# Strassen's seven products for the second product of eight chunks, a ring for x, and earlier scores

## The chip, the cores and the metric

One core of one Trainium2 chip. The metric is the device time of one execution in microseconds (us), as a median of several executions; lower is better. A run is called slow when it lies over 1.5% above the fastest of its kernel.

## The reference, cut to what matters

```python
# attention: q, k, v of shape (8, 8, 576, 64); heads 0-3 a window of 32 keys, heads 4-7 every 4th of 128
scores = scale * np.matmul(q, k.transpose(0, 1, 3, 2))
scores = np.where(masks[None], scores, -1000000000.0)
attn = softmax(scores)
x = (attn @ v).transpose(0, 2, 1, 3).reshape(4608, 512)
# two products with a squared relu between
h = x @ w_in            # (4608, 512) @ (512, 2048)
r = np.maximum(h, 0.0)
return (r * r) @ w_out  # (4608, 2048) @ (2048, 512)
```

## The kernel before

The 4608 tokens are nine chunks of 512. A chunk's first product is 64 matmuls of 128x512, each tile of it followed by a relu on ScalarE and a square on VectorE (into `g`, fp16); its second product is 64 matmuls again. Attention is done in eight "rows" b (one batch element each). From row 2 on, row b is interleaved with chunk b-1: the two products are a generator, and `pump(n)` issues n steps of it (two matmuls of 512 columns a step, 0.43 us) between small groups of attention work. In the traces an engine takes its instructions in the order of issue (below, a reciprocal of VectorE whose input was complete at 82.6 us starts at 85.41, behind four instructions issued ahead of it), so the place of a `pump` decides what waits behind what.

```python
def mm1_gen(c, g):
    xs = xT[:, :, c * TOKC : (c + 1) * TOKC]
    for ffc in range(NFF):                       # 16
        ph = pmool.tile([P, TOKC], FP32, ...)
        for dmk in range(NDM):                   # 4
            nc.tensor.matmul(ph, wi4[...], xs[:, dmk, :], ...)
            if dmk == 1: yield
        rt = osb.tile(...)
        nc.scalar.activation(rt, ph[:], ACTF.Relu)
        nc.vector.tensor_mul(g[:, ffc, :], rt, rt)
        yield

def mm2_gen(c, g):
    for t in range(TOKC // P):                   # 4 tiles of 128 tokens, 16 matmuls each
        po = pmool.tile([P, DM], FP32, ...)
        for ffc in range(NFF):
            mm2(c, g, po, t, ffc)
            if ffc % 2 == 1 and ffc < NFF - 1: yield
        store(c, t, po); yield
# ...
for b in range(2, B):
    pending.append(moe_gen(b - 1))
    last = b + 1 == B
    if not last:
        after_transposes(b)            # GpSimd waits until row b's transposes have landed
        ns = load_sliding_qk(b + 1)    # GpSimd's DMA queue
        if b == 2: cast_v(b)           # GpSimd
        dd = keep_dilated_qk(b + 1)
        load_v(b + 1)
        nr = by_token(b + 1, ns)       # GpSimd, the copy "nr<-ns"
        cast_v(b + 1)                  # GpSimd
    pump(24)
    attn_scores(b, 4)                  # 4 groups, 4 steps after each
    if not last:
        dp = keep_sliding_qk(b + 1, nr)    # SyncE's DMA queue, to DRAM
    attn_values(b, 2)                  # 9 groups, 2 steps after each
    if not last:
        transpose_dilated(b + 1, dd)   # SyncE's DMA queue
        transpose_sliding(b + 1, dp)
    pump(1000)
```

The chain that prepares the next row: the transposed keys of row b land, then GpSimd loads q and k of row b+1, copies them by token (`nr`), SyncE's queue writes them to DRAM (`dp`) and transposes them into `QKTp`, and only then can row b+1's scores begin. Row 2 holds GpSimd's casts of v for two rows, its own and row 3's.

The softmax here doesn't subtract the row's maximum and nothing guards it: scores larger than these inputs give would overflow.

## Time and profile before

The median is 322.25 us (322.08 to 323.05, three runs). The profiled execution has a span of 318.3 us. A "row of attention" below runs from the first matmul of one chunk's first product to that of the next. "Hole-free" is the row with attention and nothing that waits, 32.37 us in this trace.

| part of the trace before | us |
|---|---|
| before chunk 1 | 62.80 |
| rows 2, 3 | 32.72, 32.79 |
| rows 4, 5, 6 | 32.5, 32.8, 33.0 |
| row 7 (no work of GpSimd) | 32.37 |
| chunks 7 and 8 alone | 27.63, 27.79 |

Rows 2 to 6 together are 2.0 us longer than five hole-free rows. The prediction shows the windows of rows 3, 6 and 7. Row 2 looks like this (its window, like those of the prediction, is set about one matmul later than the first one, which changes no length by more than 0.02 us; stretch, its length, busy time and instruction count of PE, PEld, DVE, ACT, POOL, then granted clock, DMA share, GB/s):

```profile
62.98:95.70 32.72, 32.47 (x269) 17.18 (x268) 17.04 (x38) 18.36 (x32) 13.90 (x22) 1.00 1.09 230
```

GpSimd has the most to do of all rows (22 instructions), yet VectorE, with half of the row free, loses little, and neither does TensorE.

### The profile page before, as it was taken

Reading aid. Unit: us, or ns where it says so; the run is one execution under the profiler, and the core shown is the slowest. Engines: PE = TensorE matmul, PEld = TensorE weight load, DVE = VectorE, ACT = ScalarE, POOL = GpSimd, SP = SyncE. Lnnn points to the kernel's source line nnn. Section 1 sums busy time; section 2 is a strip of 40 time slices with the busy share of each in tenths; the row PEclk is TensorE's granted clock in tenths of the full one; section 3 lists DMA queues with packets and bytes.
Section 4 is the critical chain, followed back from the end, with each engine's and each line's share of the span. In section 5 each row is a group of like instructions: output and inputs, shape, how many; then the busy total and the mean of one; then the engine's idle time right before and its main releaser. Section 6 shows DMA issues by size and latency. Waiting matters only on the chain.

```text
span 318.3 us, 6260 instructions
## 1 busy us (share of the span) xinstructions
PE 302.9 (95%) x2484; PEld 157.8 (50%) x2484; DVE 162.2 (51%) x353; ACT 168.7 (53%) x286; POOL 79.2 (25%) x119
## 2 busy tenths in 40 slices
PE   1899989999999999999999999999999999999995
PEld 1455544454555445545555455555554555445542
DVE  5683548447543674369435952596256525203400
ACT  2726635568436834684368536762577256316611
POOL 4192018403480361137012800371000000000000
PEclk9999999999999999999999999999999999999999
DMA  7999998999999993998399839984810110010011
GB/s 126 197 155 215 207 210 144 195 257 192 211 259 224 205 270 100 217 194 184 106 205 184 191 91 216 191 172 126 173 44 1 68 68 0 27 72 36 1 66 66
DMA packets 79213, 46.67 MB, mean 147 GB/s; under 512 B 54352, under 2 KB 72784, under 8 KB 79184
## 3 DMA queue, kind: packets, MB, share of 16 engines
q1 hardware_dynamic: 64928, 31.60, 40.8%
q0 software_dynamic: 14256, 14.68, 28.1%
q8 instruction: 19, 0.31, 0.4%
q14 instruction: 10, 0.08, 0.1%
HBM read 39.85 MB, written 16.52 MB: 177 GB/s over the span
## 4 chain that ended last, share of the span: by engine, by line
PE 68%; DMA 12%; DVE 7%; SPq 5%; POOL 3%; issue 2%; ACT 2%; POOLq 0%; ACTq 0%
PE ph L259 31%; PE po L274 31%; SPq L120 4%; DMA wi<-in_moe_w_in_dram 4%; DVE AT L381 3%; DMA sd<-in_v_dram 2%; PE paw L452 2%; DMA sv<-in_v_dram 2%; DMA ns<-in_q_dram 2%; DVE g L270 1%; DMA out_dram<-ot 1%; PE ps L390 1%; PE pav L438 1%; DMA QKTp<-dp 1%; PE py L485 1%
## 5 line engine op out<-in xcount | busy, mean ns | idle before, releaser
L274 PE MATMUL po<-wo,g 128*128 128x512 f16 x576 | 140.8, 379 | 0.0
L259 PE MATMUL ph<-xT,wi 128*128 128x512 f16 x576 | 128.3, 380 | 0.3 <-ACT xT L491 0.3
L270 DVE TENSOR_TENSOR g<-rt 128x512 f16<-128x512 f16 x144 | 66.2, 462 | 98.5 <-ACT rt L269 98.0
L269 ACT ACTIVATE rt<-ph 128x512 f16<-128x512 f32 x144 | 85.9, 599 | 31.4 <-PE ph L259 31.0
L259 PEld LDWEIGHTS <-wi 128*128 128x128 f16 x576 | 64.1, 113 | 58.1 <-issue 0.7
L274 PEld LDWEIGHTS <-g 128*128 128x128 f16 x576 | 49.7, 97 | 46.3
L284 ACT COPY ot<-po 128x512 f32<-128x512 f32 x36 | 21.1, 587 | 54.0 <-PE po L274 51.4
L473 ACT COPY xT<-px 128x576 f16<-128x576 f16 x16 | 10.2, 639 | 31.8 <-PE px L467 31.8
L160 POOL CAST vp<-sv 128x512 f16<-128x512 f32 x24 | 16.5, 712 | 32.9 <-DMA sv<-in_v_dram 32.9
L381 DVE TENSOR_TENSOR AT<-AT,maskd 128x576 f16<-128x576 f16 x32 | 20.3, 664 | 5.3 <-ACT AT L380 4.4
L424 DVE TENSOR_TENSOR x_d<-paw,rcp_d 72x512 f16<-72x512 f32 x32 | 22.0, 687 | 1.1
L380 ACT ACTIVATE AT<-pz 128x576 f16<-128x576 f32 x32 | 18.9, 650 | 5.7 <-PE pz L409 5.6
L165 POOL CAST vd<-sd 128x512 f16<-128x512 f32 x32 | 20.9, 691 | 4.2 <-DMA sd<-in_v_dram 3.6
L381 DVE TENSOR_TENSOR AT<-AT,maskp 128x576 f16<-128x576 f16 x32 | 18.0, 568 | 5.1 <-ACT AT L380 2.8
L380 ACT ACTIVATE AT<-ps 128x576 f16<-128x576 f32 x32 | 19.0, 650 | 1.1 <-PE ps L390 1.0
L111 POOL COPY nr<-ns 128x2304 f16<-128x2304 f16 x6 | 13.0, 2161 | 25.6 <-DMA ns<-in_q_dram 25.6
L204 POOL COPY seen<-QKTp 128x1 f16<-128x1 f16 x5 | 1.3, 267 | 63.0 <-DMA QKTp<-dp 63.0
L424 DVE TENSOR_TENSOR x_p<-pav,rcp_p 96x512 f16<-96x512 f32 x24 | 16.5, 687 | 0.8
L423 DVE RECIPROCAL rcp_d<-paw 72x8 f32<-72x8 f32 x32 | 6.5, 202 | 19.5 <-PE paw L452 19.5
L452 PEld LDWEIGHTS <-AT 128*128 128x128 f16 x256 | 12.1, 98 | 8.5 <-PE px L467 1.0
L491 ACT COPY xT<-py 128x576 f16<-128x576 f16 x16 | 10.2, 640 | 10.7 <-PE py L485 10.5
L452 PE MATMUL paw<-vd,AT 128*128 128x65 f16 x256 | 13.3, 193 | 0.1
(58 smaller groups left out, 143.2 us busy)
## 6 DMA issues: line engine op xcount, KB each, us to landing
out_dram<-ot SPq DMA_DIRECT2D x32, 256.0 KB, 2.2
sv<-in_v_dram SPq DMA_DIRECT2D x40, 128.0 KB, 5.3
sd<-in_v_dram SPq DMA_DIRECT2D x8, 512.0 KB, 10.9
dp<-nr SPq DMA_DIRECT2D x12, 288.0 KB, 4.3
ns<-in_k_dram POOLq DMA_DIRECT2D x8, 288.0 KB, 6.0
ns<-in_q_dram POOLq DMA_DIRECT2D x8, 288.0 KB, 7.4
sd<-in_v_dram SPq DMA_DIRECT2D x8, 288.0 KB
wo<-in_moe_w_out_dram POOLq DMA_DIRECT2D x4, 512.0 KB, 12.9
```

Source lines behind the costliest of these rows:

```text
L111: nc.gpsimd.tensor_copy(r.rearrange("x j h d -> x h j d"), n.rearrange("x h (j d) -> x h j d", d=D))
L160: nc.gpsimd.tensor_copy(vp[b % 2][:, m : m + 2, :, 0:D], sv[:, m : m + 2, :, :])
L165: nc.gpsimd.tensor_copy(vd[b % 2][:, t, c : c + 2, :, 0:D], sd[:, t, :, D * c : D * (c + 2)].rearrange("p h (c d) -> p c h d", d=D),)
L259: nc.tensor.matmul(ph, wi4[ffc // 4][:, dmk, :, ffc % 4], xs[:, dmk, :], start=(dmk == 0), stop=(dmk == NDM - 1),)
L269: nc.scalar.activation(rt, ph[:], ACTF.Relu)
L270: nc.vector.tensor_mul(g[:, ffc, :], rt, rt)
L274: nc.tensor.matmul(po, g[:, ffc, t * P : (t + 1) * P], wo[ffc // 4][:, ffc % 4, :], start=(ffc == 0), stop=(ffc == NFF - 1),)
L284: nc.scalar.copy(ot, po)
L380: nc.scalar.activation(AT[:, u, 0:UW], ps[:, :, 0 : UW // 2], ACTF.Exp, scale=scale)
L381: nc.vector.tensor_mul(AT[:, u, 0:UW], AT[:, u, 0:UW], mask)
L424: nc.vector.tensor_tensor(out=x[0:w], in0=pv[:, :, :, 0:D], in1=rcp[0:w].unsqueeze(3).to_broadcast([w, 2, HH, D]), op=ALU.mult,)
L452: nc.tensor.matmul(pav[:, e, h * (D + 2) : h * (D + 2) + D + 1], AT[:, 4 + h, off : off + P], vd[b % 2][:, t, 2 * a + e, h, 0 : D + 1], st ...
```

## The change

The intent is an eighth fewer columns in TensorE's second product of chunks 1 to 8: Strassen's method computes a product of 2x2 blocks with seven block products in place of eight. The price is sums on VectorE. To make room, x becomes a ring of four rows and the q/k buffers shrink; the order of issue is moved as well.

```diff
-    natp = ctx.enter_context(tc.tile_pool(name="natp", bufs=4))
+    natp = ctx.enter_context(tc.tile_pool(name="natp", bufs=2))
+    otp = ctx.enter_context(tc.tile_pool(name="otp", bufs=5))
-    xT = const.tile([P, NDM, NTOK], FP16, name="xT")
+    XW = 4 * S                                          # ring of four rows, 2304 columns
+    xT = const.tile([P, NDM, XW], FP16, name="xT")
# ... in mm1_gen, after each square:
+            if c == 1 and ffc < 8:
+                next(w_sums)                            # eight sums of w_out, once
+            if sums and ffc % 4 == 3 and ffc >= HF:
+                sum_of_g(g, ffc - 3, ffc + 1)           # two sums of 1024, twice a chunk
# ... the second product (a, b, c are PSUM banks; take = ScalarE copy, add = VectorE):
+        nc.vector.tensor_sub(g[:, 0:HF, HTOK:], g[:, 0:HF, 0:HTOK], g[:, 0:HF, HTOK:])
+        yield from product(A, gq(0, 0), wq(0, 0))
+        o11 = take("u")
+        yield from product(Ck, gq(0, 1), wq(1, 0), (0,))
+        yield from product(A, sq(1), tq(1))
+        o21 = take("v")
+        yield from product(Bk, gq(1, 0), tq(2))
+        nc.vector.tensor_sub(gs[1], g[:, HF:, 0:HTOK], gs[1])
+        yield from product(A, sq(0), tq(0))
# ... (three more products, takes, adds and stores)
# ... the loop over rows:
-        pump(24)
-        attn_scores(b, 4)
+        pump(8 if b > 2 else 24)
+        attn_scores(b, 3)
         if not last:
             dp = keep_sliding_qk(b + 1, nr)
-        attn_values(b, 2)
-        if not last:
+            if b > 2:
+                transpose_sliding(b + 1, dp)
+                transpose_dilated(b + 1, dd)
+        attn_values(b, 3 if b > 2 else 2)
+        if b == 2:
+            transpose_sliding(b + 1, dp)
             transpose_dilated(b + 1, dd)
-            transpose_sliding(b + 1, dp)
         pump(1000)
```

Row 2 stays apart: its scores come at 24 steps as before, and the transposes for row 3 are issued after its values.

## The prediction

> **What bounds the kernel now.** I read the page first (engine shares, chain that ended last), then TensorE's timeline, then busy time per row of attention, and last the rows of VectorE, ScalarE, GpSimd and the DMA queue that the change loads or reorders.
>
> ```profile
> span 318.3 us, 6260 instructions
> PE 302.9 (95%) x2484; PEld 157.8 (50%) x2484; DVE 162.2 (51%) x353; ACT 168.7 (53%) x286; POOL 79.2 (25%) x119
> PE 68%; DMA 12%; DVE 7%; SPq 5%; POOL 3%; issue 2%; ACT 2%; POOLq 0%; ACTq 0%
> ```
>
> TensorE is busy 95% of the span, and the chain names it for 68%. But a busy TensorE may be one that runs below its rate, so the timeline decides: two stretches, one in a row of attention and the pure product stretch at the end (start, duration, instruction, count).
>
> ```profile
> 152.11 0.42 PE L452 MATMUL paw<-vd,AT 128*128 128x65 f16 x8
> 152.37 1.03 PE L274 MATMUL po<-wo,g 128*128 128x512 f16 x4
> 153.23 0.42 PE L467 MATMUL px<-ident,x_p 96*128 96x96 f16 x6
> 153.49 1.03 PE L274 MATMUL po<-wo,g 128*128 128x512 f16 x4
> ...
> 272.82 13.98 PE L274 MATMUL po<-wo,g 128*128 128x512 f16 x64
> 286.63 13.98 PE L259 MATMUL ph<-xT,wi 128*128 128x512 f16 x64
> ```
>
> From 272.82 to 286.63 is 13.81 us for 64 matmuls: 215.8 ns each, start to start. Eight of 65 columns take 0.26 us (32 ns each) and six of 96 take 0.26 us (43 ns), each with its own weight load. So the cost is columns at 2.4 GHz plus about 2.5 to 5 ns, and a load of 128 weights does not show even at 32 ns. TensorE is therefore at its peak from 62 us to the end, with few holes. How few, the rows tell (busy time by engine: PE, PEld, DVE, ACT, POOL):
>
> ```profile
> 95.70:128.49 32.79, 32.52 (x269) 17.09 (x268) 18.28 (x38) 18.70 (x32) 9.33 (x13) 1.00 0.90 199
> 193.80:226.80 33.00, 32.52 (x270) 17.07 (x268) 19.85 (x38) 18.69 (x32) 10.11 (x13) 1.00 0.81 171
> 226.80:259.17 32.37, 32.37 (x269) 17.16 (x268) 16.70 (x38) 18.70 (x32) 0.00 (x0) 1.00 0.23 60
> ```
>
> The last row with attention takes 32.37 us without a hole: 27.63 of the two products (two times 13.81) and 4.74 of attention. The other rows take 32.5 to 33.0; over rows 2 to 6 the holes sum to 2.0 us. GpSimd idle, VectorE does a row in 16.70 us; beside GpSimd it needs up to 19.85 for the same 38 instructions.
>
> **What the Trainium skill says.** "TensorE: Matmul & The Clock Gate", section "Back-to-back issue gap", gives N/2.4 + 2.5 ns for a warm matmul: 215.8 at 512 columns, as measured here, and 109.2 at 256. The same section also gives about 131 ns per matmul of 512 columns in a stream with weight loads; this trace contradicts that. "VectorE: DVE Perf Modes", section "The perf-mode tier table (the rule you actually need)", has 16-bit tensor_tensor from SBUF at two elements a cycle and any PSUM operand at one. The trace agrees: medians 426 ns at 512 elements and 459 at 576 are 0.52 ns an element, while the PSUM form takes 687 for 512. "SBUF — State Buffer", section "Who interferes with whom": a VectorE instruction with two SBUF inputs is blocked by a GpSimd instruction that reads SBUF. The trace agrees (minimum, median, maximum in ns; then one blocked pair):
>
> ```profile
> L381 DVE TENSOR_TENSOR AT<-AT,maskd x32: 444/459/1975, 15.1 to 245.3; 128x576 f16<-128x576 f16 x32
> ...
> 174.76 2.73 DVE L381 TENSOR_TENSOR AT<-AT,maskp 128x576 f16<-128x576 f16 x2
> ...
> 174.79 2.40 POOL L111 COPY nr<-ns 128x2304 f16<-128x2304 f16 x1 [5.64 <-DMA ns<-in_q_dram]
> ```
>
> The mask product that started with GpSimd's copy lasted as long as the copy.
>
> **The change, part by part.**
> Strassen on TensorE: of each of chunks 1 to 8, 64 matmuls of 512 columns go (13.81 us) and 7 x 2 x 8 = 112 of 256 come. At 109.2 ns these are 12.23 us. Saved 1.58 us a chunk, 12.6 us in eight. It all lies on the bound engine. This is an eighth of the columns (1.73 us) less the fixed cost of 48 more instructions. The ring of four rows is 2304 columns; only chunk 4 (2048 to 2560) wraps, so its 64 matmuls of 512 become 128 of 256: +0.16 us. Net -12.5.
>
> VectorE gains per chunk four sums of 1024 fp16 elements (0.69 us each: 426 + 0.52 x 512), two of 2048 (1.22 each) and three fp32 adds with PSUM (0.69 each): 2.8 + 2.4 + 2.1 = 7.3 us; chunk 1 also eight sums of the weights (5.5 us). In total 8 x 7.3 + 5.5 = 64, so about 226 of some 310 us: 73%, not the bound overall. In a row with GpSimd busy it is 19.5 + 7.3 = 27 of 30.8 us, however. That is close.
>
> ScalarE: four takes of 512 columns replace four copies; nothing added. PSUM: three banks are held through the second product, and the one left serves the transposes of x. The take of bank a must end before its next product: about 0.23 us to start + 0.59 + a semaphore, 0.89 against the half product of eight matmuls in between, 0.87. It should just fit: 0 to 0.05 us per occurrence.
>
> Buffers: two in place of four for the loads of q and k. Row 1's loads (22 us) need buffers last read at about 12.7, row 2's (53 us) one last read at 43.5: no delay. Up to 62 us TensorE does the same work, so the start should not change.
>
> Scores at 8 steps from row 3 on. A step is two matmuls of 512 (0.43 us). Between groups of scores lie 3 steps, 1.29 us, plus the group's 0.36: 1.65 us. ScalarE has two exponentials (0.53 start to start) and on average 1.5 relus (0.6) there, 1.96 us. It falls behind by 0.3 a group; the score banks absorb most of it, and I step through to 0.4 us of holes a row.
>
> VectorE's deadlines, stepped through from a chunk's start without GpSimd: it runs nearly without pause from 5 to 24 us. The second pair of g sums ends at 19.2, needed by the third product at 20.0; the difference of the g halves ends at 21.2, needed at 22.0. The slack is 0.8 us. GpSimd's casts and its copy have cost VectorE 1.6 to 3.2 us a row (18.3 to 19.85 against 16.70). Not all of it falls into the full stretch; what exceeds 0.8 reaches TensorE. I take 0.4 to 0.9 us for each of rows 3 to 6, on top of the 0.4 above.
>
> Row 3's transposes. In the kernel before:
>
> ```profile
> 90.07 1.15 SPq L186 DMA_DIRECT2D dp<-nr  x2
> ...
> 94.33 5.20 SPq L198 DMA_TRANSPOSE QKTd<-dd  x2
> 99.62 2.95 SPq L194 DMA_TRANSPOSE QKTp<-dp  x2
> ...
> 104.66 0.19 POOL L204 COPY seen<-QKTp 128x1 f16<-128x1 f16 x1 [10.74 <-DMA QKTp<-dp]
> ```
>
> The sliding keys landed at 104.7 while the scores wanted them at 106. Now they are wanted 8 steps into chunk 2: about 94.6 + 3.45 = 98. The new order puts the sliding transposes first. They cannot start before dp has landed (94 to 95) and the third store of chunk 1 has left (its take ends near 93.4); the second then starts near 96 and lands 3.8 us later, at 99.5. Hence a wait of TensorE of about 1.5 us, 0.5 to 3.5, in row 3 alone. Later rows issue these transposes before the second half of the row, so they land some 7 us or more ahead.
>
> Sum: -12.5; holes after: row 2 0.5, rows 3 to 6 4.6 (mean 1.15), row 7 0.4, the two pure chunks and the last add 0.3, row 3's transposes 1.5: +7.3; holes before that go: -2.0. Net -7.2, 315.0. My step-through charges every collision with GpSimd in full, and the three cuts of the schedule (8 steps, gap 3, row 2 apart) look fitted to these very waits; I lower the holes by 1 us and predict 314.0 us.
>
> **Rivals.**
> (a) TensorE's saving arrives whole: 322.25 - 12.5 + 0.5 = about 310. For it: VectorE's average load of 73%, holes of only 2 us before. Against it: 27 of 30.8 us in the middle rows.
> (b) VectorE becomes the bound of the middle rows: each sum that meets GpSimd is blocked up to 2.1 us and the third and fourth products wait. With 2 us more for each of rows 2 to 6: about 319 to 320, within 2%. For it: the 1975 ns maximum; against: GpSimd is free 20 of 33 us a row and its work may now fall elsewhere, since the earlier transposes let it start earlier.
> (c) Short matmuls do not reach 109 ns because each needs its own weights: at 122 ns Strassen gains nothing (112 x 122 = 13.7). Against: 32 ns for 65 columns with full weight loads. I give it 3%.
> (d) The earlier scores wait for their transposes in every row, 3 us each: 325. Against: only row 3's transposes are issued at the end of a row.
>
> **Range and chances.** Between (a) and (b): 310.5 to 317.5 holds it 8 times in 10. Faster by over 2% means under 315.9; 314.0 is 1.9 below that with a spread of about 2.7, so 0.73. Within 2% 0.25. Slower 0.02, only with (c) and (d) together.
>
> **What would show it.** The products of 256 columns at about 109 ns start to start in the last chunk, which should take 26.1 us in place of 27.6; at 120 the first step is wrong. Row 7 (GpSimd idle) near 31.2 us, rows 4 to 6 near 31.9; if these also take 31.0, contention was overrated. A wait of row 3's first scores on the transposes of 0.5 to 3.5 us; none, or over 5, refutes that step. Waits of the third and fourth products on VectorE's sums, under 1 us each. VectorE's busy time near 225 us. If the first 62 us change by over 1 us, the buffers were misjudged.

## The result, and the profile after

The changed kernel takes 317.84 us (316.95 to 324.38, four runs); the kernel before, run beside it, 322.16 (321.24 to 323.05). A fifth, fast run of the changed kernel (319.18) is in the ratio and not in the median. The ratio of the fast runs is 0.9869, with a 95% interval of 0.9823 to 0.9916: a gain of 1.3%, within 2%, where 314.0 and over 2% had been predicted. Here and below a ratio is the mean time of one kernel's fast runs over that of the other's fast runs of the same rounds, so it is not quite the ratio of the medians.

The profile that came with this result is of its slow run (324.38). Two repeats on two other occasions gave 0.9834 [0.9784, 0.9885] and 0.9844 [0.9792, 0.9897]; the second brought a fast trace (316.18 us, full clock), and all readings of the changed kernel below are from that one. Its page:

```profile
span 314.3 us, 7258 instructions
...
PE 292.9 (93%) x2932; PEld 202.0 (64%) x2932; DVE 217.7 (69%) x433; ACT 165.0 (52%) x286; POOL 83.8 (27%) x119
```

TensorE is busy 10.0 us less than before and the span is only 4.0 us shorter: about 6 us of the saving became idle time of TensorE. VectorE rose by 55.5 us. The rows 2, 3, 4, 6, 7 and chunk 7 alone, in the same columns as before:

```profile
63.35:98.21 34.86, 31.36 (x317) 21.79 (x316) 28.78 (x54) 19.11 (x33) 16.25 (x22) 1.00 1.10 220
98.21:132.66 34.45, 31.53 (x318) 21.56 (x317) 25.93 (x47) 18.11 (x32) 14.23 (x18) 1.00 0.95 190
132.66:164.78 32.12, 31.43 (x318) 21.43 (x317) 25.34 (x47) 17.86 (x32) 11.32 (x14) 1.00 0.94 182
196.13:227.09 30.96, 30.96 (x319) 21.68 (x317) 24.11 (x47) 17.86 (x32) 7.14 (x8) 1.00 0.79 171
227.09:257.92 30.83, 30.83 (x318) 21.84 (x317) 22.72 (x47) 17.86 (x32) 0.00 (x0) 1.00 0.11 36
257.92:283.96 26.04, 26.04 (x178) 18.19 (x177) 13.73 (x25) 11.90 (x20) 0.00 (x0) 1.00 0.12 41
```

The last two rows are what the change is worth on TensorE: 30.83 in place of 32.37, 26.04 in place of 27.63. The first two are longer than before, although the hole-free row is shorter. VectorE's busy time is 28.78 of 34.86 us in row 2, with 54 instructions instead of 38 (the eight sums of the weights fall here).

Set against the prediction, with the saving of 1.58 taken off the hole-free row (32.37 - 1.58 = 30.79) and what is above it called holes:

| us above 30.79 | before, above 32.37 | predicted | measured |
|---|---|---|---|
| row 2 | 0.35 | 0.5 | 4.07 |
| row 3 | 0.42 | 2.65 | 3.66 |
| rows 4 to 6, without the ring's wrap (0.16) | 1.2 | 3.45 | 1.90 |
| rows 2 to 6 | 2.0 | 6.6, lowered by 1 to 5.6 | 9.6 |

The sum of the holes is 4.0 us larger than predicted, and of the predicted saving of 8.25 us, 4.0 us arrived in this pair of traces. The rest of the account nearly cancels: row 7 is 0.4 us better than predicted, the part before chunk 1 is 0.55 us longer, and the two chunks alone with the end are as predicted within 0.1. Row 3's excess of 1.0 us and what rows 4 to 6 have less (1.55) more than cancel as well. So the miss is row 2, 3.6 us above its 0.5, and the 1 us by which the holes had been lowered.

What ended TensorE's waits (engine, line, what it waited for; us in total, times, longest), of the whole trace; lines whose waits all lie in the first 62 us are left out, and of the 2.8 us in the first line 0.9 lie there, so that 1.9, one wait, remain:

```profile
PE pav L547 <- DVE rcp_p L532: 2.8, 3, 1.9
PE ps L499 <- DMA QKTp<-dp: 2.2, 2, 1.3
...
PE pa L336 <- DVE gs L293: 1.5, 2, 1.1
PE px L576 <- DVE x_p L533: 0.7, 1, 0.7
```

The two largest are not where the prediction's working looked, at the third and fourth products of Strassen (`pa <- gs`, 1.5 us). They are attention's: the values product waits 1.9 us for the normalisation of an earlier one (which frees its PSUM bank), and the first scores of rows 2 and 3 wait 2.2 us for transposed keys. The first happens in row 2, with 1.25 us of the second; in TensorE's timeline (start, duration; in brackets the idle time before and what ended it):

```profile
75.13 0.43 PE L499 MATMUL ps<-QKTp 64*128 64x96 f16 x12 [1.25 <-DMA QKTp<-dp]
...
86.47 0.42 PE L547 MATMUL pav<-vp,AT 128*128 128x65 f16 x8 [1.88 <-DVE rcp_p L532]
```

And VectorE, in the same stretch:

```profile
81.50 0.69 DVE L292 TENSOR_TENSOR gs<-g 128x1024 f16<-128x1024 f16 x1
82.22 0.98 DVE L293 TENSOR_TENSOR gs<-gs,g 128x1024 f16<-128x1024 f16 x1
83.13 1.21 DVE L362 TENSOR_TENSOR g<-g 128x2048 f16<-128x2048 f16 x1
84.26 1.23 DVE L490 TENSOR_TENSOR AT<-AT,maskd 128x576 f16<-128x576 f16 x2
85.41 0.19 DVE L532 RECIPROCAL rcp_p<-pav 96x8 f32<-96x8 f32 x1
```

TensorE had finished the first values product at 82.6; its reciprocal starts at 85.41, because VectorE, in its order of issue, does two of Strassen's sums (82.22 and 83.13) and two masks first. VectorE runs without pause from 75 to 88 us here. With scores at 24 steps, the end of the scores and the start of the values lie exactly where the chunk passes from its first to its second product, and there the sums lie too. From row 3 on the scores come at 8 steps and the two do not meet in this way.

Row 3's 3.66 us are made differently: 0.93 us of waiting for keys, shown further below, and 2.0 us in three waits for VectorE. The two longest of these:

```profile
118.56 0.34 PE L576 MATMUL px<-ident,x_p 96*128 96x96 f16 x4 [0.75 <-DVE x_p L533]
...
122.00 1.05 PE L336 MATMUL pa<-wt,gs 128*128 128x256 f16 x8 [1.06 <-DVE gs L293]
```

In the microseconds before, GpSimd's copy and casts run beside VectorE: a square lasts 1.81 us in place of 0.42, and each sum of 1024 elements 0.98 in place of 0.69. By row, TensorE's waits for VectorE are 2.1 us in row 2, 2.0 in row 3 and 0.7 in rows 4 to 6 together.

One more pair of row 2 agrees with what the Trainium skill says in "SBUF — State Buffer", section "Who interferes with whom", of a VectorE instruction with two SBUF inputs that comes second to a GpSimd instruction that reads SBUF: it waits until the other is done. The sum of 2048 elements, 1.21 us above, began 0.68 us after GpSimd's copy, which ran 1.44 us more; 1.44 + 1.21 is 2.65, and the sum is recorded with 2.53 us.

```profile
89.35 2.12 POOL L119 COPY nr<-ns 128x2304 f16<-128x2304 f16 x1
...
90.03 2.53 DVE L372 TENSOR_TENSOR gs<-g,gs 128x2048 f16<-128x2048 f16 x1
```

### The profile page after: what moved, and what is told of

It reads as the page before. It is cut to its first block, busy times and chain, and to the rows that moved or that the text cites. A ratio compares the mean times of both kernels' runs of the same rounds, so it can differ in the third digit from the quotient of the medians.

```text
span 322.5 us, 7258 instructions
## 1 busy us (share of the span) xinstructions
PE 297.7 (92%) x2932; PEld 203.6 (63%) x2932; DVE 221.7 (69%) x433; ACT 164.7 (51%) x286; POOL 87.3 (27%) x119
## 4 chain that ended last, share of the span: by engine, by line
PE 61%; DVE 27%; ACT 6%; DMA 3%; issue 2%; POOL 0%; SPq 0%; POOLq 0%
PE ph L271 24%; PE pa L336 12%; PE pb L336 9%; DVE g L283 7%; DVE AT L490 6%; PE po L393 3%; DVE gs L292 3%; DVE x_p L533 3%; ACT AT L489 3%; PE pc L336 3%; DVE gs L293 3%; PE pf L433 2%; ACT rt L282 2%; DVE g L362 2%; PE paw L561 2%
## 5 line engine op out<-in xcount | busy, mean ns | idle before, releaser
L271 PE MATMUL ph<-xT,wi 128*128 128x512 f16 (+1 forms) x640 | 133.8, 359 | 0.3 <-ACT xT L600 0.3
L271 PEld LDWEIGHTS <-wi 128*128 128x128 f16 x640 | 68.4, 114 | 46.1 <-issue 0.6
L336 PEld LDWEIGHTS <-gs 128*128 128x128 f16 x384 | 36.4, 100 | 8.4 <-DVE gs L293 4.1
L336 PE MATMUL pa<-wt,gs 128*128 128x256 f16 x256 | 35.1, 282 | 2.5 <-DVE gs L293 2.4
L336 PE MATMUL pb<-wt,g 128*128 128x256 f16 x256 | 32.7, 279 | 0.8 <-DVE g L362 0.8
L349 ACT COPY ov<-pa 128x512 f32<-128x512 f32 x8 | 4.7, 585 | 30.1 <-PE pa L336 30.1
L360 DVE TENSOR_TENSOR ov<-pb,ov 128x512 f32<-128x512 f32 x8 | 5.5, 691 | 20.7 <-PE pb L336 20.7
L336 PE MATMUL pc<-wo,g 128*128 128x256 f16 x128 | 17.1, 273 | 2.8 <-DVE g L283 2.8
L490 DVE TENSOR_TENSOR AT<-AT,maskd 128x576 f16<-128x576 f16 x32 | 15.3, 503 | 3.8 <-ACT AT L489 2.8
L393 PE MATMUL po<-wo,g 128*128 128x512 f16 x64 | 17.1, 380 | 0.0
```

The lines of the kernel that those rows point to most:

```text
L271: nc.tensor.matmul(ph[:, t0:t1], wi4[ffc // 4][:, dmk, :, ffc % 4], xT[:, dmk, x0 : x0 + t1 - t0], start=(dmk == 0 and t0 == 0), stop=(dmk ...
L336: nc.tensor.matmul(banks[bank][:, t], a(k, t), b(k), start=(new and t == 0 and k == 0), stop=(k == HF - 1), skip_group_check=True,)
L393: nc.tensor.matmul(po, g[:, ffc, t * P : (t + 1) * P], wo[ffc // 4][:, ffc % 4, :], start=(ffc == 0), stop=(ffc == NFF - 1),)
L490: nc.vector.tensor_mul(AT[:, u, 0:UW], AT[:, u, 0:UW], mask)
```

## The experiments

The first theory was that the loss sits in row 2 alone, where Strassen's sums and GpSimd's casts and copy meet on VectorE, so that taking either away, or the plain product in chunk 1, would bring the predicted time. The first four runs did not bear that out. The second theory, which the later runs test, is that there are two waits, each hiding the other: (1) in row 2 VectorE's order of issue, with Strassen's sums ahead of attention's masks and normalisations, holds up TensorE; (2) row 3's scores cannot begin before the chain of GpSimd and DMA has delivered their keys, a moment that does not move when TensorE gets there sooner. Rivals: the eight sums of the weights alone cause row 2's loss (W); the reordering by itself costs what is missing; GpSimd's blocking of VectorE in every row sets the time (the prediction's rival (b)); and TensorE's saving does not arrive at all.

All twelve runs, with rows from their traces (holes as above, over 5 x 30.79 + 0.16 = 154.1 us for rows 2 to 6; for kernels with plain products in a chunk 1.58 more for each):

| run | median us (range, n) | ratio to before [95%] | rows 2, 3 | rows 4 to 6 | holes of rows 2 to 6 |
|---|---|---|---|---|---|
| changed kernel again, first | 317.00 (315.73–328.58, 7) | 0.9834 [0.9784, 0.9885] | slow trace | | |
| changed kernel again, second | 316.27 (316.17–318.06, 4) | 0.9844 [0.9792, 0.9897] | 34.86, 34.45 | 94.43 | 9.6 |
| chunk 1 plain | 316.94 (314.39–351.74, 6) | 0.9810 [0.9752, 0.9868] | slow trace | | |
| no GpSimd casts and copy in row 2 | 316.03 (314.49–316.49, 4) | 0.9799 [0.9743, 0.9855] | 35.94, 33.51 | 95.14 | 10.5 |
| no sums | 317.07 (312.41–318.73, 4) | 0.9746 [0.9659, 0.9832] | 31.86, 38.12 | 92.62 | 8.5 |
| no sums of the weights | 316.92 (315.31–318.04, 4) | 0.9842 [0.9794, 0.9891] | 33.61, 35.61 | 94.67 | 9.8 |
| no sums, row 3 at 24 | 308.79 (308.09–310.23, 4) | 0.9590 [0.9526, 0.9654] | 31.30, 31.94 | 93.83 | 3.0 |
| schedule alone | 325.14 (321.82–327.86, 4) | 1.0118 [1.0047, 1.0189] | 33.16, 34.62 | 97.25 | 3.2 |
| row 3 at 12 | 315.64 (314.38–319.56, 6) | 0.9790 [0.9739, 0.9842] | 34.57, 32.49 | 96.59 | 9.5 |
| chunk 1 plain, row 3 at 12 | 315.50 (314.08–318.24, 6) | 0.9797 [0.9745, 0.9850] | 32.37, 33.45 | 96.15 | 6.3 |
| row 3 at 12, casts on ScalarE | 314.79 (313.37–317.19, 6) | 0.9789 [0.9744, 0.9835] | 35.74, 32.08 | 93.59 | 7.3 |
| chunk 1 plain, row 3 at 12, casts on ScalarE | 313.23 (310.80–314.37, 6) | 0.9724 [0.9678, 0.9770] | 33.47, 34.22 | 93.56 | 5.6 |

The kernel before had medians of 321.78 to 321.88 beside them. The medians and ranges hold every run; slow runs, which the ratios leave out, were one of the seven of the first repeat, two of six with chunk 1 plain, two of four without sums, and one each of the schedule alone and of row 3 at 12. The rows are from one trace each; the ratio decides.

### The changed kernel again

No edit.

> The changed kernel once more, to have fast runs and, with luck, a trace of the fast state. Theory L (the loss lies in row 2, where VectorE is blocked by GpSimd's casts and copy while masks, squares and the sums of g come together, and the hole lets the clock drop): row 2 of attention (chunk 1) takes 34 to 37 us in a fast run against 40.8 in the slow profile, the half-clock stretch being shorter or absent; every other row as in the slow profile within 0.3 us. Rival M (the loss is spread over all rows, the profile's row 2 is an accident of the slow run): row 2 near 32 and the other rows longer than 32. Time 317 to 318 either way.

> The changed kernel once more on the chip of these runs, to compare within one chip and for a trace of the fast state: 316 to 318 us in fast runs; row 2 of 34 to 37 us where the clock is 0.99 or more.

The first repeat's trace was slow again (328.58 us, mean clock 0.977), so it explains nothing here; its other runs lie at 315.7 to 318.3. The second gave the fast trace used above, with row 2 at 34.86 us, within the 34 to 37 expected.

### Chunk 1 with the plain second product

```diff
-        yield from mm1_gen(c, g, True)
-        yield from mm2_strassen_gen(c, g)
+        yield from mm1_gen(c, g, c > 1)
+        yield from (mm2_strassen_gen if c > 1 else mm2_gen)(c, g)
...
-        attn_scores(b, 3)
+        attn_scores(b, 3 if b > 2 else 4)
```

> Strassen for chunks 2 to 8 only; chunk 1 (row 2) has the plain second product and the old gap of 4 steps, the sums of the weights stay in chunk 1. Gives up 1.58 us of TensorE's saving. Theory L: row 2 back to about 32.7 us, no half clock in any run, 315.5 to 316.5 us, so faster than the changed kernel by 1 to 2 us and with no slow runs. Rival M: 1.5 us slower than the changed kernel, about 319.

This gives up 1.58 us of TensorE's saving in row 2 and takes the pressure off VectorE there. It came out at 0.981, no worse than the changed kernel and not separated from it. Strassen in chunk 1 is thus worth nothing that the runs can show. The expectation that no slow run would come failed: two of six were slow, and one, the profiled one, took 351.74 us at a granted clock of 0.854 over nearly its whole length. That trace is not used.

### No GpSimd casts and copy in row 2

```diff
-            if b == 2:
-                cast_v(b)
...
-            nr = by_token(b + 1, ns)
-            cast_v(b + 1)
+            if b in (2,):
+                nr = ns
+            else:
+                nr = by_token(b + 1, ns)
+                cast_v(b + 1)
```

Its output is wrong (the values of two rows are missing and the tokens unordered).

> Wrong result on purpose: in row 2 GpSimd makes no casts of v and no copy of q and k (the next rows work on stale data of the same shapes); VectorE's, ScalarE's and TensorE's instructions are all there. Theory L: row 2 near 31.5 us, no waits of TensorE on VectorE over 1 us in it, 312 to 314 us. Rival V (VectorE's own work is too much in row 2, with scores late at 24 steps, whatever GpSimd does): row 2 stays at 34 or more, 316 to 318.

Missed: row 2 did not shrink (35.94 us). Its timeline on TensorE:

```profile
75.23 0.43 PE L501 MATMUL ps<-QKTp 64*128 64x96 f16 x12 [2.02 <-DMA QKTp<-dp]
75.60 2.75 PE L273 MATMUL ph<-xT,wi 128*128 128x512 f16 x6
...
87.25 0.43 PE L549 MATMUL pav<-vp,AT 128*128 128x65 f16 x8 [1.06 <-DVE x_p L535]
```

Two things are to be seen. The values still wait for VectorE, 1.06 us, with GpSimd out of the way, so VectorE's own work is enough for a wait; that contention makes the rest of the 1.88 us is likely, but two single traces whose rows began differently do not show it. And the wait on the first transposes was longer (2.02), after which six matmuls took 2.75 us in place of 1.49: the granted clock from 75 to 79 us was 0.57. So this run has a different hole in the same row, and the two cannot be set off against each other. That GpSimd's work in row 2 is what the changed kernel loses by does not hold: the ratio (0.9799) is not separated from the changed kernel's.

### No sums on VectorE

```diff
-            if c == 1 and ffc < 8:
-                next(w_sums)
-            if sums and ffc % 4 == 3 and ffc >= HF:
-                sum_of_g(g, ffc - 3, ffc + 1)
...
-        nc.vector.tensor_sub(g[:, 0:HF, HTOK:], g[:, 0:HF, 0:HTOK], g[:, 0:HF, HTOK:])
...
-        nc.vector.tensor_sub(gs[1], g[:, HF:, 0:HTOK], gs[1])
```

The buffers of the sums are filled once with zeros; the result is wrong.

> Wrong result on purpose: all sums of g and of the weights are taken from VectorE (the tiles are zeroed once in chunk 0); TensorE's matmuls and the three adds per chunk stay. The prediction's first step (112 matmuls of 256 columns save 1.58 us a chunk): TensorE's saving arrives almost whole, 310.5 to 312.5 us, row 2 near 31.3. If the saving itself were smaller than 12.5 us in sum, 315 or more.

Missed, and it is the run that taught most. Row 2 is nearly free of holes (31.86). But row 3 grew to 38.12:

```profile
104.30 0.67 PE L495 MATMUL ps<-QKTp 64*128 64x96 f16 x12 [4.80 <-DMA QKTp<-dp]
104.90 2.75 PE L271 MATMUL ph<-xT,wi 128*128 128x512 f16 x6
```

TensorE reaches row 3 some 2.3 us sooner (at 95.9 instead of 98.2) and then waits 4.80 us for keys that land at 104.3, later than in the changed kernel's trace (102.7). What follows runs at half rate (2.75 us for six; the granted clock from 102 to 108 us was 0.57). Of the 9.6 us of holes only 1.1 went: what was removed in row 2 came back in row 3, as 3.9 us more of waiting for keys and then some 2.6 us of low clock, less the 2.0 us of waits for VectorE that had been there. Only two of the four runs were fast, and the other one took 312.41 us where the traced one took 315.69, so the size of this loss differs from run to run.

### No sums, and row 3's scores at 24 steps

The edit before, and this one:

```diff
-        pump(8 if b > 2 else 24)
+        pump({2: 24, 3: 24}.get(b, 8))
```

> Wrong result on purpose, as the kernel without sums, but row 3's scores come at 24 steps as row 2's do. That kernel lost 4.8 us in row 3 waiting for the transposes and some 2.5 more at half clock. Theory D (up to row 3's scores a chain of GpSimd and DMA work sets the time; a row 2 without holes only turns into a wait of row 3): the wait is gone or under 0.5 us, row 3 takes 30.8 to 31.3 us, and the time is 2 to 5 us under that kernel's: about 310 to 312, TensorE's saving of 12.5 us nearly whole. Rival (row 3 loses for another reason, the transposes are merely what came last): row 3 stays at 34 or more.

Rows 2 and 3 in the columns of the windows above:

```profile
62.60:93.90 31.30, 31.03 (x317) 21.88 (x316) 18.26 (x40) 18.95 (x33) 13.40 (x21) 1.00 1.07 221
93.90:125.90 32.00, 31.03 (x319) 21.95 (x318) 19.29 (x42) 17.73 (x31) 9.75 (x15) 1.00 1.08 207
```

Both rows lie within 1.2 us of 30.8, the holes of rows 2 to 6 fall to 3.0 us, and the time to 308.79, 13 us below the kernel before: Strassen's saving on TensorE (12.5 us predicted) arrives whole here. The time was better than expected, though row 3 (31.94) stayed above its 30.8 to 31.3. The edit takes the sums out of every row, so it removes VectorE's waits in rows 3 to 6 as well as the two in question. Zeros in the buffers did not change the clock to speak of (0.998 against 1.000). Against the run without sums alone the ratio falls from 0.9746 to 0.9590, for one number in one `pump`. The two causes are therefore not additive: without the sums alone the gain over the changed kernel is about 2.8 us and not separated (0.9746 against 0.9834), with both it is about 8.

### The schedule alone

The kernel before, with the plain product, the large buffers and the whole x, and the loop of the changed kernel:

```diff
-        pump(24)
-        attn_scores(b, 4)
+        pump(8 if b > 2 else 24)
+        attn_scores(b, 3)
         if not last:
             dp = keep_sliding_qk(b + 1, nr)
+            if b > 2:
+                transpose_sliding(b + 1, dp)
+                transpose_dilated(b + 1, dd)
-        attn_values(b, 2)
-        if not last:
+        attn_values(b, 3 if b > 2 else 2)
+        if b == 2:
+            transpose_sliding(b + 1, dp)
             transpose_dilated(b + 1, dd)
-            transpose_sliding(b + 1, dp)
```

> The kernel before with nothing but the new schedule: scores at 8 steps from row 3 on, gap 3, the new order of the transposes. No Strassen, so no sums on VectorE. Theory D: row 2 near 32.7 us, row 3 waits 1.5 to 5 us for its transposes and then runs for some us at half clock, so 35 to 38 us; rows 4 to 7 near 32.4; 323 to 326 us, slower than before by 2 to 4 us. Rival (the schedule costs nothing by itself, only Strassen's sums do): 321.5 to 322.5.

The reordering by itself costs 1.2% (1.0118 [1.0047, 1.0189]), as expected. Part of it is row 3's wait, with no Strassen anywhere:

```profile
101.95 0.43 PE L391 MATMUL ps<-QKTp 64*128 64x96 f16 x12 [2.14 <-DMA QKTp<-dp]
102.31 1.49 PE L260 MATMUL ph<-xT,wi 128*128 128x512 f16 x6
```

Its expectation for row 3 (35 to 38 us) was too high: after this wait of 2.14 us the matmuls kept their rate (1.49 us for six). The profiled run was the fastest of the four, so its trace shows only 1.2 us of the 3.8. In size the rival that the reordering costs what is missing is thus close to the 4 us. But in this trace rows 4 to 7 take 32.42 us each and wait for nothing, and the run without sums and with row 3 at 24 keeps the new order there and is 13 us faster than the kernel before; what costs in the order is row 3's early scores. The changed kernel with its sums and row 3 at 24 steps, which would show the two side by side, was not run.

### Row 3's scores at 12 steps, with Strassen everywhere and with chunk 1 plain

Two runs of working kernels. Both have this edit; the second has that of the chunk 1 run as well.

```diff
-        pump(8 if b > 2 else 24)
+        pump({2: 24, 3: 12}.get(b, 8))
...
-            if b > 2:
-                transpose_sliding(b + 1, dp)
-                transpose_dilated(b + 1, dd)
+            transpose_sliding(b + 1, dp)
+            transpose_dilated(b + 1, dd)
         attn_values(b, 3 if b > 2 else 2)
-        if b == 2:
-            transpose_sliding(b + 1, dp)
-            transpose_dilated(b + 1, dd)
```

> The changed kernel with row 3's transposes ahead of row 2's values and its scores at 12 steps; Strassen in chunk 1 as well. Theory L: row 2 keeps its hole and half clock (35 to 41 us), row 3 gains the 1 to 2 us of its waits: 315 to 317 us, 1 us under the changed kernel, and slow runs stay. Rival (the row 3 wait is the whole loss): 312 to 313.

> An attempt at a better kernel: chunk 1 with the plain second product (no hole in row 2), row 3's transposes issued ahead of row 2's values, so not behind the stores of chunk 1, and row 3's scores at 12 steps. By theories L and D together row 2 takes 32.7 us, row 3 31.5 to 32.5 without a wait over 0.7 us, the rest as in the changed kernel: 313 to 315 us. If holes remain in row 3, 316 to 317.

With Strassen everywhere, row 3's wait for its keys is gone and row 3 takes 32.49 us. Rows 4 to 6 give back 2.2 us, in waits for VectorE (2.5 us in place of 0.7), so the holes of rows 2 to 6 are 9.5 against 9.6, and the ratio, 0.979, is not separated from the changed kernel's. With chunk 1 plain the holes fall to 6.3, of which 1.6 is paid for with the plain product; 0.9797, the same time, just outside the expected 313 to 315. Row 3 (33.45) missed its 31.5 to 32.5: no wait for keys, but 2.1 us of waits for VectorE.

### Casts of v on ScalarE

The edit of row 3 at 12 steps, and the casts of rows 3 to 7 moved to the end of the values on ScalarE (row 2's own casts stay on GpSimd); once with Strassen everywhere, once with chunk 1 plain.

```diff
             nr = by_token(b + 1, ns)
-            cast_v(b + 1)
...
         attn_values(b, 3 if b > 2 else 2)
+        if not last:
+            cast_v_on_scalar(b + 1)
```

> The kernel with row 3's transposes early and its scores at 12 steps, and in addition the casts of v for the next row (seven a row, from row 2 on) run on ScalarE after the values instead of on GpSimd; VectorE's work is the same. Theory L (GpSimd's reads block VectorE, whose slack the sums have used up): rows 3 to 6 near 31.2 us against 31.7 to 33.2 in that kernel, row 2 33 to 34, VectorE's busy time down by 5 us or more, 312.5 to 314.5 us. Rival V (VectorE's own work makes the holes): rows unchanged within 0.3 us, 315 to 316, or longer by ScalarE's 4.2 us a row.

> The same with the plain second product in chunk 1. Row 2 near 32.4 us, row 3 31.5, rows 4 to 6 31.2: 311.5 to 313.5 us under theory L. Under rival V as the plain-chunk-1 kernel before it, 315 to 316.

With Strassen everywhere, rows 3 to 6 are together 3.4 us shorter than with the casts on GpSimd, but row 2 is not: its values still waited 2.62 us for VectorE, and after that wait the granted clock was 0.64 and 0.51 from 86 to 88 and from 88 to 90 us. The gain in time is not separated (0.9789 against 0.979), and 314.79 just misses the expected 312.5 to 314.5.

```profile
85.34 0.42 PE L557 MATMUL pav<-vp,AT 128*128 128x65 f16 x8 [2.62 <-DVE rcp_p L542]
...
86.87 1.91 PE L346 MATMUL pb<-wt,g 128*128 128x256 f16 x8
```

Eight matmuls of 256 columns take 1.91 us here, where they take 1.04 at full clock: part of row 2's hole in this trace is clock. With chunk 1 plain, rows 2 and 3 are

```profile
63.50:96.90 33.40, 32.37 (x269) 17.15 (x268) 21.17 (x46) 19.66 (x34) 10.19 (x15) 1.00 1.08 221
96.90:131.20 34.30, 31.64 (x318) 21.81 (x317) 24.04 (x46) 22.46 (x42) 5.34 (x6) 1.00 0.98 197
```

with VectorE's load in row 2 down from 28.78 to 21.17 us and GpSimd's from 16.25 to 10.19. Both rows are longer than expected (32.4 and 31.5; row 3 waits 0.6 us for keys and 1.5 for VectorE), so that the time hit its range was partly luck. At 313.23 us and 0.9724 [0.9678, 0.9770] it is the fastest working kernel: it beats the kernel before by 2.8%, and the changed kernel, run on the same chip, by 1.2% (0.9724 / 0.9844; the intervals do not overlap). Against the version with Strassen everywhere they do overlap, and the two single traces show equal sums of rows 2 and 3 (67.7 and 67.8), so which of the two edits brought how much stays open.

### No sums of the weights

```diff
-            if c == 1 and ffc < 8:
-                next(w_sums)
+            if c == 0 and ffc < 8 and ffc % 2 == 0:
+                nc.vector.memset(wt[ffc // 2][:], 0.0)
```

Its output is wrong, which doesn't matter for the time.

> Wrong result on purpose: of the changed kernel only the eight sums of the weights are taken from VectorE (their tiles are zeroed in chunk 0). Theory L: VectorE has caught up with these sums before row 2's scores begin, so nothing changes: 316 to 318 us, row 2's hole stays. Rival W (the sums of the weights, which fall into row 2 alone, make its hole): row 2 near 32 us, 312 to 314.

0.9842 against 0.9844 for the changed kernel in the same rounds. In the trace row 2 is 1.25 us shorter and row 3 1.16 us longer, once more one hole exchanged for the other. The rival that the eight sums in chunk 1 are the cause falls.

## Why the prediction was wrong, point by point

**What held.** Strassen on TensorE: 16 matmuls of 256 columns take 1.75 us (109.4 ns each; 109.2 predicted), as chunk 7 shows:

```profile
271.73 1.91 PE L336 MATMUL pa<-wo,g 128*128 128x256 f16 x16
273.48 1.04 PE L336 MATMUL pc<-wo,g 128*128 128x256 f16 x8
```

Chunk 7 takes 26.04 us (26.1 predicted). Row 7 takes 30.83, under the 31.2 predicted: the 0.4 us a row given to ScalarE falling behind did not come there. Rival (c), short matmuls at 122 ns, is out. VectorE's sums cost 0.69 and 1.21 us (0.69 and 1.22 predicted), its busy time is 217.7 us (near 225). The first 62 us grew by 0.55 us. The third product's waits were to be under 1 us; the longest was 1.06. Rival (d) is out too: after row 3 no wait for keys stands in the trace. Neither rival (a) nor (b) came: the saving did not arrive whole, and GpSimd's blocking did not cost 2 us in each of rows 2 to 6, as rows 4 to 6 hold 1.9 us in all, less than predicted. It is not nothing either: with the casts on ScalarE rows 3 to 6 were 3.4 us shorter. The holes of rows 3 to 6 apart from the keys sum to 4.6 us, as predicted, but by luck: 2.7 of them lie in row 3 alone, where 1.15 had been put.

One reading of the prediction is not right as it stands. Its line of 2.73 us at 174.76 is two mask products: the first began before GpSimd's copy and took its usual 0.46 us, the second began 0.52 us after the copy and lasted 2.19, until 0.31 after the copy's end. It is the second that was blocked.

**What failed.** The step is the list of holes, in its term "row 2 0.5". It measured 4.1. The prediction stepped through VectorE's deadlines for rows with scores at 8 steps, found a slack of 0.8 us, and gave row 2, which keeps its scores at 24 steps, half a microsecond without any working of its own. But the row that had not been moved is the one where the new sums fall between the scores and the values: the first values product waited for its normalisation behind two sums and two masks, which the timelines of VectorE and TensorE show instruction by instruction. Removing the sums removed row 2's hole (31.86 us); removing GpSimd's work alone, or the weights' sums alone, did not bring a gain. What was not tested is whether the order alone would do, the normalisations issued ahead of the sums: VectorE has no pause from 75 to 88 us, so the sums might then have been late for their own products, and order and amount of work are not told apart. About 1 us of row 2 (a wait of 1.25 for its first keys, 0.25 before) is something else: it was 0 to 2.0 us in runs with the same code up to there, and its cause was not looked for further.

**A step that hit for another reason.** Row 3's wait for its keys was predicted at 1.5 us and measured 0.93. Yet the keys landed about 3 us later than the predicted 99.5. SyncE's queue issued the transposes at 97.32, after three stores of chunk 1, the last at 96.62:

```profile
96.62 0.37 SPq L354 DMA_DIRECT2D out_dram<-ox  x1
97.32 3.07 SPq L202 DMA_TRANSPOSE QKTp<-dp  x2
...
102.75 0.43 PE L499 MATMUL ps<-QKTp 64*128 64x96 f16 x12 [0.93 <-DMA QKTp<-dp]
```

The stores are not what held them. With row 3 at 12 steps the transposes stand ahead of the stores and were issued no earlier:

```profile
97.16 2.76 SPq L202 DMA_TRANSPOSE QKTp<-dp  x2
```

There the queue waited 4.8 us for `dp`, the keys on their way to DRAM, and without the sums, behind the stores again, 1.8 us. So the term that was off is the landing of `dp`, put at 94 to 95 us: its two halves, issued from 91.5 on, took 4.1 and 6.0 us. The wait of TensorE stayed short only because row 2 had already lost the time, so that TensorE asked for the keys at 101.8 us, 3.8 later than planned. Two errors of about the same size hid each other, and the hit was luck. With row 2 repaired (no sums) the wait is 4.80 us, outside the predicted 0.5 to 3.5.

**The holes as a sum.** The prediction added the holes up as if each could be had or removed by itself, and then lowered them by 1 us in the belief that the schedule had been fitted to the waits. The runs show that the holes hang together: 9.6 us in the changed kernel, 8.5 without the sums, 9.5 with row 3 moved to 12 steps, 3.0 with the sums gone and row 3 at 24. Without the sums, what row 2 gave came back as row 3's wait for keys; with row 3 moved, what row 3 gave came back in rows 4 to 6 as waits for VectorE. The lowering had no ground: the schedule by itself costs 1.2%.

**Where the expected gain went.** TensorE's saving of some 12.5 us is there in full (308.79 us without the sums and with row 3 at 24). About 7.6 us of it, the growth of the holes from 2.0 to 9.6 in rows 2 to 6, became new holes. In the traces TensorE's named waits for VectorE grew there from 1.0 to 4.8 us (rows 2 and 3 above all) and those for keys from 0.25 to 2.2 (rows 2 and 3); the other 2 us stand under no wait that the profile names.

**What stays open.** Some executions of the changed kernel are slow (324.38 and 328.58 us). Their traces show row 2 at about 41 us, with holes and then granted clocks near half for some 10 us (0.55 and 0.53 from 86 to 97 us in the first, 0.51 from 90 to 100 us in the second). In both, GpSimd's copy lay earlier in row 2 than in the fast traces, beside a square that lasted 2.39 us in the first and 3.43 us in the second. That this is the cause is argued from few traces, not shown. Nor was the run at a clock of 0.854 explained.

## What to carry to other kernels

When a change moves work onto a second engine, step through that engine's order of issue in every stage, and first of all in the stages that the change leaves in their old order, because there the new work can land ahead of something urgent. Before adding up expected waits, ask for each what would happen to it if the ones before it vanished: here row 2 became 3.0 us shorter and row 3's wait for its keys 3.9 us longer. And test such pairs together, since neither removed alone brought a gain that the runs separate, while both together were worth about 8 us.

## What the Trainium skill lacked or had wrong

- "TensorE: Matmul & The Clock Gate", section "Back-to-back issue gap", gives about 131 ns for each matmul of 512 columns in a stream with weight loads and calls N/2.4 + 2.5 the gap of an isolated one. Here the streams run at 215.8 ns (512 columns) and 109.4 ns (256), as the second formula says.
- The same page, section "HAM oscillation — how this bites in real kernels", states the rule that TensorE should have no idle gap above about 3.4 us. Here a single wait of 2.02 us was followed by six matmuls in 2.75 us in place of 1.49, at a granted clock of 0.57, and one of 2.62 us by a clock of 0.64 and then 0.51, while waits of 2.14 and 2.12 us in other runs were followed by the full clock: no fixed length of one wait separates them.
- The same page, section "Seeing it yourself", in its note on the peak-current limiter, says that one or two busy cores never trip it. One run of this one-core kernel had a granted clock of 0.854 over almost all of a span of 349.9 us. What the chip's other cores did then is not known, nor whether it was this limiter, so this contradicts the page only if they were idle and it was.
